# Two more blocks by seven products, and a block's second layer cut by unit halves, on one Trainium2 core

## The chip, the cores and the metric

The kernel runs on one core of a Trainium2 chip. Five engines matter: PE multiplies matrices and writes to PSUM, ACT and DVE do elementwise work and empty PSUM, POOL and SP here mostly issue DMAs. Each engine takes its own queue in order, and semaphores hold an instruction until what it needs is there. The metric is device time in microseconds (us) of one execution, as a median over runs.

## The reference

A gated recurrence over 6144 steps for each of 4 sequences and 256 channels, then a layer that takes the larger of two products and projects back:

```python
sig = 1.0 / (1.0 + np.exp(-f_logit))
f = lower_bound + (1.0 - lower_bound) * sig
h = f[:, t] * h + (1.0 - f[:, t]) * x[:, t]      # for each t; y[:, t] = h
g = np.maximum(y @ w1, y @ w2)                    # 256 -> 1024 units
out = g @ w_out                                   # 1024 -> 256
```

There are 24576 tokens in all, in fp32.

## The kernel before

**Algebra.** The larger of two products is written as max(a, b) = a + relu(b - a). So the first layer needs one product alone, with wd made from w2 - w1, and a ReLU; the part that stays linear goes through w13 = w1 w_out, a 256 x 256 matrix, added in the second layer. The factor of the recurrence's input (`om`, one minus the lower bound) is folded into the weights: `scale_w1` scales a half of w1, `half_w1` casts it to 16 bits, `make_wd` forms a quarter of wd, `turn_w1` and `keep_w1T` transpose the scaled w1 through PSUM, `make_w13` multiplies it by w_out (tile `wob`).

**Blocks.** Tokens are cut into 48 blocks of 512, the unit of all loops. A block has two SBUF tiles `r` (`rts[j, 0]` and `rts[j, 1]`), each with four 128-unit slices of the hidden layer and one slice with half of the recurrence's output y. The recurrence of a block: `gate` (sigmoid on ACT), `decay`, `drive` and two `scan`s on DVE, each scan starting from the end of the block before. `first_layer(j, fc)` makes unit slice fc with two matmuls of 512 columns; after each second slice ACT writes the ReLU of both to the `r` tile (L442). Its PSUM tile `dT` has two buffers of two banks each; all other PSUM tiles (`ps`) share four buffers of one bank.

**Second layer, direct.** `second_layer(j, slot)` issues an eighth of a block's 40 matmuls of 256 columns (L480): for each of four token groups two for y with w13 and eight for the units with w_out, y first. ACT or DVE copies the result out of PSUM (L489) and SP stores it.

**Second layer by sevens.** From block 4 on, two blocks are taken together as a 2 x 2 block product that needs seven products instead of eight: `sevenths(p)` lists 7 x 20 matmuls of 128 columns for pair p. For it DVE forms four sums of `r` tiles a pair (`sum1` to `sum4`, L499), and once four sums of weights (`make_sevens`). Products X, B and E are accumulated in PSUM banks; ACT copies one bank into another (`seed`), takes snapshots, and ACT or DVE writes the results (`leave`).

**Order.** The whole order is written by hand. Before the loop over pairs come the loads, the weights, and blocks 0 to 3 with their recurrences, each block's second layer set between the first-layer slices of the next. In the loop over p each of 16 slots issues a first-layer slice of pair p, then 8.75 of the list's matmuls of pair p - 1, and what `seq` and `gates` have due: scans and gates for pair p + 1, sums for p and p - 1. The list starts two slots late (`LAG`), in p = 3, so that 17.5 of a pair's matmuls are always left over to the next.

**Queues.** SP issues the first loads, the four weight loads, all stores, and `cross(c)`, the transposing loads of a chunk of 1024 tokens from a 16-bit scratch. POOL issues the casting loads: w_out, chunks 1 to 3 in natural layout (PE transposes them), and from chunk 4 on `fetch`, which writes the scratch; after `cross(c)` POOL waits for its first tile and then fetches chunk c + 1. POOL's first wait is `pool_waits(w1n[0])`: w_out and the fetches behind it are issued when the first half of w1 has landed.

## Time and profile before

| what | value |
|---|---|
| median of 5 runs | 378.79 us (378.07 to 380.32) |
| the profiled execution | 378.51 us |
| its span, first to last instruction | 376.7 us |
| PE busy | 369.4 us, 98% |
| DVE busy | 337.9 us, 90% |
| ACT busy | 303.2 us, 80% |
| granted clock of PE | 0.999 |
| w_out, issue to landing | 6.2 us |
| four loads of w1 and w2, issue to landing | 5.9 / 6.6 / 7.4 us (least, median, most) |

The span is the profiled execution from its first to its last instruction; the time also has 1.8 us around it. Busy shares are means over all stages. "Chain" means the work that ended last, followed back at each step to what released it. In a timeline row the first number is the start in us from the span's start, the second the time from the first start to the last end of a run of equal instructions; brackets hold the engine's idle time before it and what ended it. A matmul's duration includes the way through the array, so equal matmuls start closer together than they last.

### The profile page before, as it was taken

To read this page: it belongs to the slowest core of one execution; us is meant where nothing else is said; L and a number is where in the kernel's file an instruction comes from. 1 tells how busy PE (TensorE), PEld (TensorE's weight loads), DVE (VectorE), ACT (ScalarE), POOL (GpSimd) and SP (SyncE) were. 2 spreads that over 40 slices of the span, in tenths; PEclk is the share of its full clock that TensorE was granted. 3 is DMA by queue.
4 is the path that set the end of the run, shared out by engine and by line. 5 is a ranking of instruction groups with operands and counts; after the bars stand their busy time and mean duration, and the time that the engine had idled before them with its cause. 6 is when DMAs were issued, how large, how long until landed. Compare 5 with 4: busy or idle time off the path is not lost.

```text
span 376.7 us, 9634 instructions
## 1 busy us (share of the span) xinstructions
PE 369.4 (98%) x4156; PEld 281.9 (75%) x4156; DVE 337.9 (90%) x408; ACT 303.2 (80%) x412; POOL 36.8 (10%) x80
## 2 busy tenths in 40 slices
PE   7999999999999999999999999999999999999995
PEld 6777767777777777777777777777777777777784
DVE  5796889999999999999999999999999999999762
ACT  5866798888888798798888888887988888888752
POOL 1401100110110100110100201100101210000000
PEclk9999999999999999999999999999999999999999
DMA  7999989999999999998999979999989989920223
GB/s 264 241 198 247 220 155 201 212 214 214 264 203 205 250 177 227 260 180 224 276 150 244 278 141 235 298 160 234 278 143 252 278 159 229 229 114 2 114 113 112
DMA packets 104543, 77.17 MB, mean 205 GB/s; under 512 B 93298, under 2 KB 95348, under 8 KB 103796
## 3 DMA queue, kind: packets, MB, share of 16 engines
q1 hardware_dynamic: 101536, 51.19, 59.3%
q0 software_dynamic: 2544, 25.17, 34.8%
q8 instruction: 32, 0.52, 0.6%
q10 hardware_dynamic: 420, 0.20, 0.2%
q14 instruction: 11, 0.09, 0.1%
HBM read 53.48 MB, written 48.23 MB: 270 GB/s over the span
## 4 chain that ended last, share of the span: by engine, by line
PE 96%; DMA 2%; ACT 1%; SPq 0%; DVE 0%; issue 0%; DVEq 0%
PE ps L643 45%; PE dT L434 44%; PE ps L480 5%; DMA r<-in_moe_w_dram 2%; PE ps L174 1%; PE ps L390 0%; SPq L117 0%; ACT r L345 0%; ACT S L349 0%; PE ps L376 0%; DVE osb L561 0%; DVE osb L582 0%; ACT sn L574 0%; PE dT L643 0%; DVEq L561 0%
## 5 line engine op out<-in xcount | busy, mean ns | idle before, releaser
L442 ACT ACTIVATE r<-dT 128x1024 f16<-128x1024 f32 x192 | 195.9, 1023 | 53.5 <-PE dT L434 53.3
L434 PE MATMUL dT<-r,wd 128*128 128x512 f16 x768 | 225.0, 379 | 0.0
L643 PEld LDWEIGHTS <-S 128*128 128x128 f16 x1760 | 115.5, 101 | 37.2 <-DVE S L499 0.2
L643 PEld LDWEIGHTS <-r 128*128 128x128 f16 x1320 | 90.9, 101 | 36.8 <-issue 0.2
L224 DVE TENSOR_TENSOR_SCAN r<-ff,r,v 128x512 f16<-128x512 f16 x88 | 108.2, 1270 | 0.8
L643 PE MATMUL ps<-t,S 128*128 128x128 f16 x1320 | 101.6, 219 | 0.0
L499 DVE TENSOR_TENSOR S<-r 128x2560 f16<-128x2560 f16 x44 | 65.4, 1486 | 15.3 <-ACT r L442 15.3
L434 PEld LDWEIGHTS <-wd 128*128 128x128 f16 x768 | 67.6, 113 | 4.6 <-DVE wd L358 0.5
L643 PE MATMUL ps<-wob,r 128*128 128x128 f16 x704 | 69.9, 219 | 0.0
L499 DVE TENSOR_TENSOR S<-r,S 128x2560 f16<-128x2560 f16 x44 | 64.9, 1475 | 0.0
L279 ACT ACTIVATE u<-fT 128x512 f16<-128x512 f16 x88 | 56.1, 638 | 0.0
L207 DVE TENSOR_SCALAR ff<-u,nom 128x512 f16<-128x512 f16 (+1 forms) x98 | 31.6, 345 | 9.1 <-ACT u L201 3.1
L643 PE MATMUL ps<-w,r 128*128 128x128 f16 x176 | 38.5, 219 | 0.0
L341 POOL CAST waited<-fT 128x1 f32<-128x1 f16 x22 | 10.5, 477 | 275.5 <-DMA fT<-scr 275.5
L643 PE MATMUL ps<-t,r 128*128 128x128 f16 x430 | 34.1, 219 | 0.1
L561 DVE TENSOR_TENSOR osb<-ps,sn 128x512 f32<-128x512 f32 x44 | 30.1, 684 | 3.2 <-PE ps L643 3.2
L643 PE MATMUL ps<-wob,S 128*128 128x128 f16 x352 | 32.6, 219 | 0.0
L217 DVE TENSOR_TENSOR v<-u,xT 128x1024 f16<-128x1024 f16 x44 | 30.1, 684 | 0.0
L549 ACT COPY sn<-ps 128x512 f32<-128x512 f32 x44 | 25.8, 586 | 2.0 <-PE ps L643 2.0
L559 ACT COPY osb<-ps 128x512 f32<-128x512 f32 x43 | 25.1, 583 | 0.8 <-PE ps L643 0.8
L480 PEld LDWEIGHTS <-r 128*128 128x128 f16 x160 | 16.0, 101 | 6.6
L643 PE MATMUL ps<-w,S 128*128 128x128 f16 x88 | 19.3, 219 | 0.0
(58 smaller groups left out, 136.4 us busy)
## 6 DMA issues: line engine op xcount, KB each, us to landing
out_dram<-osb SPq DMA_DIRECT2D x46, 512.0 KB, 3.8
scr<-in_f_logit_dram POOLq DMA_DIRECT2D x22, 512.0 KB, 7.5
scr<-in_x_dram POOLq DMA_DIRECT2D x22, 512.0 KB, 10.0
r<-in_moe_w_dram SPq DMA_DIRECT2D x4, 512.0 KB, 6.6
fT<-in_f_logit_dram POOLq DMA_DIRECT2D x3, 256.0 KB, 8.2
xT<-in_x_dram POOLq DMA_DIRECT2D x3, 256.0 KB, 8.8
out_dram<-osb SPq DMA_DIRECT2D x3, 256.0 KB, 2.5
osb<-in_f_logit_dram SPq DMA_DIRECT2D x2, 256.0 KB, 3.7
```

What stands on the lines that cost most here:

```text
L207: nc.vector.tensor_scalar(out=ff[:, h, cols], in0=u[:, h, cols], scalar1=nom[:, h : h + 1], scalar2=1.0, op0=ALU.mult, op1=ALU.add,)
L217: nc.vector.tensor_tensor(out=like(v[:, :, cols], xT), in0=like(u[:, :, cols], xT), in1=xT, op=ALU.mult,)
L224: nc.vector.tensor_tensor_scan(out=y_of(j, h), data0=ff[:, h, o : o + TB], data1=v[:, h, o : o + TB], initial=0.0 if t0 == 0 else y_of(j - ...
L279: nc.scalar.activation(out=mids[p + NBLK, "u"][:, h, cols], in_=held[c, 0][:, h, cols], func=AF.Sigmoid, scale=-1.0,)
L434: nc.tensor.matmul(dT[:, fc % 2, :], lhsT=wd[:, kc, unit_cols(fc)], rhs=y_of(j, kc), start=(kc == 0), stop=(kc == KC - 1),)
L442: nc.scalar.activation(out=rts[j, k][:, g - 1 : g + 1, :].rearrange("p q (i m) -> p q i m", m=P), in_=dT[:].rearrange("p q (m i) -> p q i ...
L480: nc.tensor.matmul(ps[:, r, :], lhsT=left, rhs=right, start=(s == 0 and r == 0), stop=(s == n - 1 and r == 1), skip_group_check=True,)
L499: nc.vector.tensor_tensor(out=t[:], in0=a, in1=b, op=op)
L549: nc.scalar.copy(out=t[:], in_=bank[b][:])
L559: nc.scalar.copy(out=dst, in_=bank[b][:])
L561: nc.vector.tensor_tensor(out=dst, in0=bank[b][:], in1=snap[name][:], op=ALU.add)
L643: nc.tensor.matmul(bank[b][:, i, :], lhsT=a[:, k, cols], rhs=w, start=fresh, stop=after is not None, skip_group_check=True,)
```

## The change

- Blocks 2 and 3 become a pair of their own (p = 1) in the list of sevens, and are worked off beside the first layer of blocks 4 and 5 (p = 2). The list starts after one slot, so 8.75 matmuls are left over to each next pair instead of 17.5. Pair 1 has no seed: X is snapshotted, B gets a bank of its own, and DVE adds the snapshot at the end. The scans of blocks 4 to 7 move in the order.
- Block 1's second layer is set beside the first layer of blocks 2 and 3 (five and three pieces).
- w_out is loaded by two DMAs into two tiles, and POOL waits for the second cast of the first load (`raws[1, 1]`) instead of w1.
- Block 0's second layer is issued by unit halves into one PSUM tile `dT` that it keeps until the end (`second_first`): units 0 and 1 of all four token groups, then 2 and 3, later 4 to 7 and y. Its first layer for units 4 to 7 is made one by one in `ps` tiles (`first_single`), with ReLUs on ACT for 4 and 7 and on DVE for 5 and 6. ACT copies the four groups out at once.
- Scaling the second half of w1 moves from ACT to DVE; the two turns of w1 are further apart.

```diff
@@ -315,7 +314,7 @@
     lbr = const.tile([KC, P], FP32)
     waited = const.tile([P, 1], FP32)
     warm = const.tile([P, 1], FP32)
-    wob = wpool.tile([P, FC, D], HALF)
+    wob = [wpool.tile([P, KH, D], HALF, name=f"wob{g}") for g in range(2)]
     wd = wpool.tile([P, KC, DFF], HALF)
     w1T = wpool.tile([P, FC, D], HALF)
     w13 = wpool.tile([P, KC, D], HALF)
...
@@ -340,9 +339,9 @@
     def pool_waits(t):
         nc.gpsimd.tensor_copy(out=waited[:], in_=t)
-    def scale_w1(g):
+    def scale_w1(g, mul):
         for kc in range(KC):
-            nc.scalar.mul(w1s[g][:, kc, :], w1n[g][:, kc, :], om[:, kc : kc + 1])
+            mul(w1s[g][:, kc, :], w1n[g][:, kc, :], om[:, kc : kc + 1])
     def half_w1(g, copy):
         for kc in range(KC):
...
@@ -446,6 +445,29 @@
                 in_=dT[:].rearrange("p q (m i) -> p q i m", m=P),
                 func=AF.Relu,
             )
+
+    def first_single(fc, relu):
+
+        k, g = divmod(fc, KH)
+        dT = ps_o.tile([P, TB], FP32, name="ps")
+        for kc in range(KC):
+            nc.tensor.matmul(
+                dT[:],
+                lhsT=wd[:, kc, unit_cols(fc)],
+                rhs=y_of(0, kc),
+                start=(kc == 0),
+                stop=(kc == KC - 1),
+            )
+        relu(
+            out=rts[0, k][:, g, :].rearrange("p (i m) -> p i m", m=P),
+            in_=dT[:].rearrange("p (m i) -> p i m", m=P),
+        )
+
+    def relu_act(out, in_):
+        nc.scalar.activation(out=out, in_=in_, func=AF.Relu)
+
+    def relu_dve(out, in_):
+        nc.vector.tensor_scalar_max(out=out, in0=in_, scalar1=0.0)
     def store(j, osb, groups=slice(0, TB // P), cols=slice(0, D), queue=None):
         b, t0, nb, c, o = blocks[j]
...
@@ -486,11 +508,41 @@
                 skip_group_check=True,
             )
             if r == 1 and s == n - 1:
-                (nc.scalar.copy if j in (0, 3) else nc.vector.tensor_copy)(
+                (nc.vector.tensor_copy if j else nc.scalar.copy)(
                     out=osb[:, 2 * g : 2 * g + 2, :], in_=ps[:]
                 )
                 if i == ns - 1:
                     store(j, osb)
+
+    def second_first(i, fcs):
+
+        ns = TB // P
+        g, r = divmod(i, 2)
+        if "first" not in acc:
+            acc["first"] = ps_d.tile([P, 2, TB], FP32, name="dT")
+        ps = acc["first"][:, g, r * D : (r + 1) * D]
+        toks = slice(i * P, (i + 1) * P)
+        end = fcs[-1] == FC - 1
+        terms = [
+            (rts[0, fc // KH][:, fc % KH, toks], wob[fc // KH][:, fc % KH, :])
+            for fc in fcs
+        ]
+        terms += [(y_of(0, s)[:, i:TB:ns], w13[:, s, :]) for s in range(KC) if end]
+        for n, (left, right) in enumerate(terms):
+            nc.tensor.matmul(
+                ps,
+                lhsT=left,
+                rhs=right,
+                start=(fcs[0] == 0 and r == 0 and n == 0),
+                stop=(end and n == len(terms) - 1),
+                skip_group_check=True,
+            )
+        if end and i == ns - 1:
+            osb = opool.tile([P, ns, D], FP32, name="osb")
+            nc.scalar.copy(
+                out=osb[:].rearrange("p (g r) d -> p g (r d)", g=2), in_=acc["first"][:]
+            )
+            store(0, osb)
     sums = {}
...
@@ -601,8 +653,11 @@
         def given(t):
             return lambda k: t[:, k, :]
+
+
+        begin = p == PAIR0 - 1
         product("X", part(0, 0), plain(0, lo), True)
-        then(seed("B", "X"))
+        then(snapshot("X", 1) if begin else seed("B", "X"))
         product("E", sub(1), given(t1), True)
         then(snapshot("E", 5))
         if end:
...
@@ -623,8 +678,8 @@
         else:
             product("X", sub(2), given(t2))
             then(snapshot("X", 2))
-            product("B", part(0, 1), plain(1, lo))
-            then(leave("B", ja, lo, None, False))
+            product("B", part(0, 1), plain(1, lo), begin)
+            then(leave("B", ja, lo, 1 if begin else None, False))
             product("X", sub(3), given(t3))
             then(leave("X", jb, hi, 5, False))
             product("E", sub(4), plain(1, hi))
...
@@ -662,14 +717,6 @@
         fetch_first(1)
         for g in range(NG):
             fetch_w(g)
-        pool_waits(w1n[0][:, 0, 0:1])
-        nc.gpsimd.dma_start(
-            out=wob[:].rearrange("p (g q) c -> p g (q c)", g=NG),
-            in_=moe_w_out.rearrange("(g p q) c -> p g (q c)", g=NG, q=NQ),
-        )
-        for c in range(1, 5):
-            for s in range(2):
-                fetch(c, s)
         wt = ps_d.tile([P, 2, 2 * TB], HALF, name="dT")
         lbc = ps_d.tile([P, TB], FP32, name="dT")
...
@@ -694,81 +741,91 @@
         warm_up(8)
         first_bf16(1, 0, nc.scalar.copy)
         first_bf16(1, 1, nc.scalar.copy)
+        pool_waits(raws[1, 1][:, 0, 0:1])
+        for g in range(NG):
+            nc.gpsimd.dma_start(
+                out=wob[g][:].rearrange("p q c -> p (q c)"),
+                in_=moe_w_out[g * NQ * P : (g + 1) * NQ * P, :].rearrange(
+                    "(p q) c -> p (q c)", q=NQ
+                ),
+            )
+        for c in range(1, 5):
+            for s in range(2):
+                fetch(c, s)
         first_turn(1, 0)
         first_turn(1, 1)
         first_recurrence(1)
         warm_up(24)
-        scale_w1(0)
+        scale_w1(0, nc.scalar.mul)
         half_w1(0, nc.scalar.copy)
-        scale_w1(1)
         pt0 = turn_w1(0)
         for pair in range(2):
             make_wd(0, pair)
             for fc in range(2 * pair, 2 * pair + 2):
                 first_layer(0, fc)
+        scale_w1(1, nc.vector.tensor_scalar_mul)
         half_w1(1, nc.vector.tensor_copy)
-        pt1 = turn_w1(1)
         for pair in range(2):
             make_wd(1, pair)
-            for fc in range(4 + 2 * pair, 6 + 2 * pair):
-                first_layer(0, fc)
         keep_w1T(0, pt0)
-        keep_w1T(1, pt1)
+        for fcs in ((0, 1), (2, 3)):
+            for i in range(TB // P):
+                second_first(i, fcs)
+        keep_w1T(1, turn_w1(1))
+        first_single(4, relu_act)
+        first_single(5, relu_dve)
+        first_single(6, relu_dve)
         steps = turn_steps(1)
-        make_w13(0)
         turn(steps[:8])
         gate(1)
+        first_single(7, relu_act)
+        make_w13(0)
+        turn(steps[8:])
         make_w13(1)
-        turn(steps[8:])
         for step in scan_steps(1):
             step()
         cross(4)
-        for fc in range(FC):
-            if fc == 4:
-                turn(turn_steps(2))
-                gate(2)
-            if fc == 6:
-                first_layer(1, 0)
-                first_layer(1, 1)
-            if fc < 7:
-                second_layer(0, fc)
+        last = tuple(range(KH, FC))
+        steps = turn_steps(2)
+        second_first(0, last)
+        turn(steps[:8])
+        gate(2)
+        second_first(1, last)
+        second_first(2, last)
+        turn(steps[8:])
+        second_first(3, last)
         for step in scan_steps(2):
             step()
         for step in make_sevens():
             step()
-        for fc in range(2, FC):
+        for fc in range(FC):
             first_layer(1, fc)
             if fc == 3:
-                second_layer(0, 7)
-        turn(turn_steps(3))
+                turn(turn_steps(3))
         gate(3)
         cross(5)
-        early = scan_steps(3)
+        for step in scan_steps(3):
+            step()
+        scans = {PAIR0: pair_scans(PAIR0)}
+        part = 0
         for fc in range(FC):
             first_layer(2, fc)
-            second_layer(1, fc)
-            if fc < 4:
-                early[fc]()
+            if fc in (1, 2, 4, 5, 7):
+                second_layer(1, part)
+                part += 1
+            if fc > 3:
+                pair_gate(PAIR0, fc - 4)
+        for t in ("decay0", "drive0", "scan00", "scan01"):
+            scans[PAIR0][t]()
         cross(6)
-        scans = {PAIR0: pair_scans(PAIR0)}
-        gates = {0: 0, 1: 1, 4: 2, 5: 3}
-        order = {
-            2: ("decay0", "drive0"),
-            3: ("scan00",),
-            4: ("scan01",),
-            6: ("decay1",),
-            7: ("drive1",),
-        }
         for fc in range(FC):
             first_layer(3, fc)
-            second_layer(2, fc)
-            if fc in gates:
-                pair_gate(PAIR0, gates[fc])
-            for t in order.get(fc, ()):
-                scans[PAIR0][t]()
+            if fc in (1, 2, 4):
+                second_layer(1, part)
+                part += 1
+        sum3(1)
         queue, due = [], 0
-        pieces3, piece = (1, 3, 5, 9, 11, 13, 15), 0
         for p in range(PAIR0, NPAIR):
             first = p == PAIR0
             more = p + 1 < NPAIR
...
@@ -777,31 +834,30 @@
                 (36, scans[p]["scan11"]),
                 (112, lambda: sum3(p)),
             ]
+            if first:
+                seq += [(9, scans[p]["decay1"]), (10, scans[p]["drive1"])]
             if more:
                 scans[p + 1] = pair_scans(p + 1)
                 seq += [
-                    (64, scans[p + 1]["decay0"]),
-                    (66, scans[p + 1]["drive0"]),
-                    (70, scans[p + 1]["scan00"]),
-                    (84, scans[p + 1]["scan01"]),
+                    (73 if first else 64, scans[p + 1]["decay0"]),
+                    (75 if first else 66, scans[p + 1]["drive0"]),
+                    (79 if first else 70, scans[p + 1]["scan00"]),
+                    (93 if first else 84, scans[p + 1]["scan01"]),
                     (131, scans[p + 1]["decay1"]),
                     (133, scans[p + 1]["drive1"]),
                 ]
-            if not first:
-                seq += [
-                    (9, lambda: sum1(p - 1)),
-                    (18, lambda: sum2(p - 1)),
-                    (50, lambda: sum4(p - 1)),
-                ]
-                queue += sevenths(p - 1)
+            seq += [
+                (0 if first else 9, lambda: sum1(p - 1)),
+                (18, lambda: sum2(p - 1)),
+                (50, lambda: sum4(p - 1)),
+            ]
+            queue += sevenths(p - 1)
             seq.sort(key=lambda e: e[0])
-            gates = {4: 0, 6: 1, 12: 2, 14: 3} if more else {}
+            gates = {5 if first else 4: 0, 7 if first else 6: 1, 12: 2, 14: 3}
+            gates = gates if more else {}
             for slot in range(2 * FC):
                 first_layer(2 * p + slot // FC, slot % FC)
-                if first and slot in pieces3 or p == PAIR0 + 1 and slot == 1:
-                    second_layer(2 * PAIR0 - 1, piece)
-                    piece += 1
-                if p > PAIR0 + 1 or (p == PAIR0 + 1 and slot >= LAG):
+                if p > PAIR0 + 1 or slot:
                     due += NSEV / (2 * FC)
                     while due >= 1:
                         due -= 1
```

The remaining hunks put `wob[fc // KH][:, fc % KH, :]` where `wob[:, fc, :]` stood.

More of the change, by code (lines that the diff above doesn't have):

```diff
@@ L38 @@
     CH = 1024
-    LAG = 2
     NSEV = 7 * 4 * 5
@@ L392, in make_w13 @@
                 lhsT=w1T[:, fc, kc * P : (kc + 1) * P],
-                rhs=wob[:, fc, :],
+                rhs=wob[fc // KH][:, fc % KH, :],
                 start=(fc == 0),
@@ L403, in right @@
     def right(k, cols):
-        return wob[:, k * KH : (k + 1) * KH, cols], w13[:, k, cols]
+        return wob[k][:, :, cols], w13[:, k, cols]
     def make_sevens():
@@ L478, in second_layer @@
                 fc = s - KC
-                left, right = rts[j, fc // KH][:, fc % KH, toks], wob[:, fc, :]
+                left, right = rts[j, fc // KH][:, fc % KH, toks], wob[fc // KH][:, fc % KH, :]
             nc.tensor.matmul(
```

## The prediction

> **What bounds the kernel now.** I read the page's busy shares first, then the chain that ended last, then the timeline of the first 36 us and of the last 15, then busy time by stretches.
>
> ```profile
> span 376.7 us, 9634 instructions
> PE 369.4 (98%) x4156; PEld 281.9 (75%) x4156; DVE 337.9 (90%) x408; ACT 303.2 (80%) x412; POOL 36.8 (10%) x80
> PE 96%; DMA 2%; ACT 1%; SPq 0%; DVE 0%; issue 0%; DVEq 0%
> ```
>
> The matmul engine is the chain: from 11.5 us it has next to no gap until the last sums. So a change counts in two ways: by the matmuls that it removes, and by the waits that it puts in front of PE. The prices come from the chain's pieces in order of time (start, length, what):
>
> ```profile
> 11.50 1.73 PE dT L434 x8
> 21.28 1.09 PE ps L480 x10
> 58.77 0.50 PE ps L643 x9
> ```
>
> A 512-column matmul costs 0.216 us, a 256-column one 0.1095, a 128-column one 0.0557 (the last from a pair's 14.72 us less its 32 of 512: 7.80/140). The rows that feed PE, from the timeline, where the first number is the start and the second the duration:
>
> ```profile
> 8.64 0.87 POOL L666 DMA_DIRECT2D wob<-in_moe_w_out_dram  x1
> 12.13 0.75 DVE L349 CAST S<-r 128x512 f16<-128x512 f32 x2
> 12.40 1.94 ACT L442 ACTIVATE r<-dT 128x1024 f16<-128x1024 f32 x2
> 12.80 1.66 DVE L358 SCALAR_TENSOR_TENSOR wd<-r,om 128x256 f16<-128x256 f32 x4
> 14.39 1.28 DVE L382 COPY w1T<-ps 128x1024 f16<-128x1024 f16 x2
> ...
> 363.50 1.49 DVE L499 TENSOR_TENSOR S<-r 128x2560 f16<-128x2560 f16 x1
> ...
> 365.04 1.13 PEld L643 LDWEIGHTS <-S 128*128 128x128 f16 x20 [0.17 <-DVE S L499]
> ```
>
> The last row says that the final pair's product E already waits for its sum. And busy time by stretches of 5 us (after the length: PE, PEld, DVE, ACT, POOL with instruction counts, then granted clock, DMA share, GB/s):
>
> ```profile
> 10.00:15.00 5.00, 4.85 (x38) 3.08 (x36) 5.00 (x14) 4.53 (x7) 3.51 (x7) 1.00 1.10 246
> 15.00:20.00 5.00, 5.00 (x52) 4.27 (x51) 2.76 (x6) 3.10 (x5) 0.49 (x1) 1.00 1.12 209
> 35.00:40.00 5.00, 5.00 (x38) 3.74 (x37) 2.33 (x5) 4.05 (x6) 0.00 (x0) 1.00 0.71 127
> 50.00:55.00 5.00, 5.00 (x33) 3.29 (x32) 4.92 (x7) 4.82 (x7) 0.00 (x0) 1.00 0.68 117
> ```
>
> Over the nine stretches from 10 to 55 us DVE idles 8.7 us in all and ACT 10.2: that is the room for new side work.
>
> **The change, part by part.** I stepped the queues of PE, ACT and DVE through the order in which each program issues, with the rows' spacings: first-layer pair 0.87 on PE; ReLU of two units 0.92 apart on ACT; sums 1.40, scans 1.19 apart on DVE; 0.2 from a matmul's issue to its reader. The old order, stepped so, ends PE at 372.2; the trace has its last matmuls end there (371.49 + 0.72).
>
> 1. Matmuls. Blocks 2 and 3 cost 80 matmuls of 256 columns, 8.76 us; as sevens 140 of 128, 7.80. Gain 0.96. Block 0's second layer keeps its 40.
>
> 2. w_out. Its DMA leaves POOL after the cast that ends at 7.42 instead of after the first weight lands at 8.47. One issue of 128 rows takes 0.56 (the fetches behind it), so the halves are issued from about 7.65 and 8.2, and the eight fetches behind them 0.8 earlier. In the packet records w_out first moves at 10.87, 2.2 after its issue; so now at about 9.6. The four weight loads land at 8.47, 9.73, 11.00 and 12.34, so some 600 KB of them are still to come, chiefly w2's second half. Bounds for its landing: 12.34 if w_out yields, 16.3 if w_out goes wholly first (3.94 us from its first packet to its landing at 14.81). Where both overlap, about 11.2 to 11.5 us, a quarter microsecond holds 19 packets of w_out and 12 of the loads: neither goes first, so I take one for one: 300 packets of 2 KB at 0.08 + 0.17 us on 16 engines, 4.7 us, less the 0.2 or so that packets overlap: about 14.5. Half 0 of w_out then lands by some 12.5, ahead of its use at 13.4. Behind the new wait in POOL's queue stand both halves and the fetches; block 1's first transpose at 17.3 waits for them last, and since the same bytes go the same way, its tile still lands near 16.0. Were it late, PE would stand still by as much.
>
> The Trainium skill, "DMA: Bandwidth & Descriptors", section Queues, rings and completion order, says that each DMA engine takes turns between the queues it has work for, packet by packet. That agrees with these counts and speaks against an earlier w_out; by the rule the sum would be the one below, and without contention 0.7 less.
>
> 3. Weights of units 4 to 7. The two scalings move from ACT (0.72 each) to DVE. No row shows that operation on DVE; 0.35 (L207's 16-bit form) and 0.68 (L561) bound it, the cast L349 at 0.41 reads the same tile shape, so 0.41. DVE: wd of half 0 ends 12.15, scaling 12.97, cast 13.65; the second wd could start there and now waits for 14.5: 0.85 late, to 16.1; w1T copies 16.7 and 17.4 (L382, 0.64 each).
>
> 4. PE meanwhile: first layer of units 0 to 3 ends at 13.0. It used to go on with transposes; now block 0's second layer needs the ReLU of units 0 and 1, which ends at 13.42 (12.40 + 1.02): wait 0.41 with the second one's. Then 16 matmuls, transposes, units 4 and 5. Unit 6 needs a PSUM buffer that the first w1T copy frees, block 1's transposes the second's, unit 7 and w13 the buffers of units 5 and 6, whose ReLUs are on DVE (no row has it; L489 copies as much from PSUM in 0.68, 0.61 apart, L207 16-bit data in 0.35: I take 0.62, the PSUM row). Waits 0.34, 0.20, 0.17, 0.19 = 0.90 (0.22 with weights in time). The tail of block 0 waits 0.12 for w13's second copy (L397, 0.37).
>
> 5. Buffers. Block 0's accumulator holds one of the two first-layer PSUM buffers until ACT has copied it (nearest row L442, 1.02; 0.58 for half the size). Units 2 and 3 of block 1 wait 0.38 for it. Behind that copy ACT has four ReLUs and a gate in a row: first layer of block 2 waits 0.37, and of block 4 another 0.37, since block 3's stage has 3 pieces of second layer beside 8 units and so runs at ACT's pace.
>
> 6. Pair 1's sums. DVE gains four sums (5.6), three additions (1.8), scalings and ReLUs (2.1), and loses two output copies (1.2): some 8.3 us more by 58 us, against 8.7 idle. It is then full: sum 2 is 0.17 late for its product, y of block 5 0.13, and sum 1 of pair 2 0.44.
>
> 7. The loop. The list of sevens now runs 8.75 matmuls closer to its sums. In a steady pair sum 1 ends at 144.36 and E starts at 146.18; one slot earlier leaves 0.9 us, so nothing waits. ACT's seed becomes a snapshot of the same size once. At the end 9 matmuls instead of 18 cover the last sum, so the 0.11 there becomes 0.61: 0.50 lost. Transposing loads, their SP queue (block 1's store goes behind chunk 6's load; its buffer is next needed 8 us later) and the fetches are hidden: chunk 5 lands at 43.1, its gate is due near 46; beyond 3 us of delay the next pair's scans, then its first layer, would slip.
>
> Sum: waits 0.41 + 0.90 + 0.12 + 0.38 + 0.37 + 0.37 + 0.74 + 0.50 = 3.79; less 0.96; less 0.6 of small waits that the same stepping puts into the old order between 12 and 19 us and that go: **+2.2 us**. The profiled execution took 378.51 (span 376.7 and 1.8 around it); with the sum 380.7. It lies 0.3 below the median 378.79, so I forecast 381.0.
>
> **Rivals.**
> - Weights in time (half 1 of w2 by 13.65): point 4 loses 0.7, sum +1.5, 380.3. For it: w_out's packets may start later than 9.6. Against: they need a delay of over a microsecond.
> - w_out first: landing 16.3, unit 4 itself waits; +4.0, 382.8. The counts in the overlap speak against it.
> - Not slower: ACT hides the hand-overs. If ReLU and copy leave their buffers early enough, the waits of points 4 and 5 (2.18) and of 6 (0.74) do not form, and -0.96 + 0.50 gives 378.3. It decides at 1.6 us of new waits ahead of the tail (I have 2.7 there after the 0.6 taken off): below that the time is not slower by 0.3%, about what a measurement here can tell. For it: ACT idles 1.9 us from 15 to 20 and 2.7 from 30 to 35 now. Against: the order puts each ReLU directly before its reader at 13.4, and DVE's 2.7 idle us from 35 to 40 are spent by point 6.
> - DVE never catches up: later than 0.9 us in every pair, E waits each time. At 0.1 a pair 2 us more, 383. DVE is 95% busy in the loop, with 0.56 idle before sum 3 in each pair; that works the lag off in about three pairs, so I hold it unlikely.
>
> **How the numbers follow.** Late weights with all waits 0.40; weights in time 0.27, of which 0.07 ends inside 0.3%; w_out first or a lasting lag 0.10; waits mostly hidden 0.23, of which 0.16 inside 0.3% and 0.07 faster by more. So slower 0.70, the same 0.23, faster 0.07: the saving itself is 0.96, under the 1.14 that counts. The range 378.9 to 383.0 reaches from half-hidden waits to w_out first.
>
> **What would show it.** After: PE with gaps at 13.0 (released by ACT's ReLU), 16 to 18.7 (DVE's copies and ReLUs), near 25 and 29 (ACT); wd of half 1 starting near 14.5 after an idle of DVE released by a weight DMA; DVE over 4.8 of 5 us in each stretch from 20 to 55; PE waiting 0.6 for the last sum 1. If PE has under 1.6 us of new gaps before 60 us, I am wrong.

## The result and the profile after

The changed kernel takes 380.17 us (median of 22 runs, 379.43 to 381.62) against 378.57 for the kernel before on the same chip (41 runs, 377.85 to 380.52): a ratio of 1.004, 95% interval 1.003 to 1.0051. Its profiled execution took 380.4 us, span 378.5; 1.9 more than the one of before. The predicted 381.0 was 0.8 high, the range 378.9 to 383.0 holds the result, and the sign is the predicted one.

From the page of the changed kernel: the span, the busy shares and the chain that ended last.

```profile
span 378.5 us, 9765 instructions
PE 369.5 (98%) x4216; PEld 281.5 (74%) x4216; DVE 345.6 (91%) x417; ACT 302.2 (80%) x411; POOL 41.2 (11%) x81
PE 94%; DMA 3%; ACT 1%; SPq 0%; DVE 0%; issue 0%; POOL 0%; DVEq 0%
```

PE issues 60 matmuls more (140 small ones for 80 larger) and is as busy as before, yet its last matmul ends at 374.04 instead of 372.21 us, 1.83 later. The chain gives up two points of PE, one of them to DMA: on the page it now leads through the landing of w_out (2%). The busy time of PE includes some of a wait, since a matmul counts until it leaves the array, so below a **gap** is the time between the starts of two matmuls less the spacing of that shape (0.0557, 0.1095 or 0.2165 us). Bracketed idle time in a row is about 0.16 shorter than the gap.

The timeline of the changed kernel (start, duration, engine and line, what, and in brackets the idle time before it with what ended it):

```profile
7.67 1.22 POOL L746 DMA_DIRECT2D wob<-in_moe_w_out_dram  x2
...
8.92 1.34 ACT L344 ACTIVATE r<-r,om 128x512 f32<-128x512 f32 x2 [0.96 <-DMA r<-in_moe_w_dram]
...
11.98 0.88 DVE L344 TENSOR_SCALAR r<-r,om 128x512 f32<-128x512 f32 x2
...
12.83 1.94 ACT L441 ACTIVATE r<-dT 128x1024 f16<-128x1024 f32 x2 [1.54 <-PE dT L433]
13.44 1.67 DVE L357 SCALAR_TENSOR_TENSOR wd<-r,om 128x256 f16<-128x256 f32 x4
...
14.15 1.91 PE L532 MATMUL dT<-wob,r 128*128 128x256 f16 x16 [0.50 <-DMA wob<-in_moe_w_out_dram]
...
17.41 1.29 DVE L470 TENSOR_SCALAR r<-ps 128x512 f16<-128x512 f32 x2 [0.17 <-PE ps L454]
...
24.50 1.01 ACT L542 COPY osb<-dT 128x1024 f32<-128x1024 f32 x1 [1.39 <-PE dT L532]
...
25.56 1.02 PE L433 MATMUL dT<-r,wd 128*128 128x512 f16 x4 [0.24 <-ACT osb L542]
...
29.45 1.02 PE L433 MATMUL dT<-r,wd 128*128 128x512 f16 x4 [0.25 <-ACT r L441]
...
41.14 1.02 PE L433 MATMUL dT<-r,wd 128*128 128x512 f16 x4 [0.25 <-ACT r L441]
...
42.03 1.49 DVE L551 TENSOR_TENSOR S<-r 128x2560 f16<-128x2560 f16 x1 [0.31 <-ACT r L441]
...
366.87 1.13 PEld L698 LDWEIGHTS <-S 128*128 128x128 f16 x20 [0.17 <-DVE S L551]
```

Four things are to be seen. The predicted hand-overs stand at 14.15, 25.56, 29.45 and 41.14, the first released by w_out and not by the ReLU (which ended at 13.85). The second `wd` starts at 13.44 with no wait for a weight. DVE idles for 0.31 us ahead of pair 1's sum 1, until ACT's ReLU is done. And the last pair's product E waits 0.17 for its sum, exactly as before: nothing was lost at the end.

Busy time by stretches of the changed kernel (PE, PEld, DVE, ACT, POOL, then clock, DMA share, GB/s):

```profile
10.00:15.00 5.00, 3.76 (x30) 2.30 (x28) 5.00 (x13) 3.23 (x5) 2.58 (x5) 1.00 1.11 243
...
25.00:30.00 5.00, 4.51 (x33) 2.64 (x32) 4.72 (x11) 4.08 (x5) 0.00 (x0) 1.00 0.57 65
30.00:35.00 5.00, 5.00 (x35) 3.46 (x33) 3.70 (x5) 4.68 (x7) 1.15 (x3) 1.00 1.41 311
...
40.00:45.00 5.00, 4.75 (x46) 3.11 (x44) 4.69 (x7) 3.95 (x5) 1.04 (x2) 1.00 1.04 194
```

PE loses time in the stretches of those hand-overs, at an undisturbed clock. DVE is busy 4.9 us more over 10 to 55 us, and still idles 1.3 us in one stretch (30 to 35): it is fuller, not full.

All gaps of PE, term by term as the prediction set them up:

| term | predicted | measured |
|---|---|---|
| matmuls | -0.96 | -0.96 |
| before block 0's second layer | 0.41 | 0.66 at 13.3 us |
| DVE's copies and ReLUs, 16 to 18.7 us | 0.90 | 0 |
| w13's second copy | 0.12 | 0.08 at 21.2 |
| block 0's accumulator | 0.38 | 0.40 at 25.0 |
| ReLU before block 2 | 0.37 | 0.41 at 28.8 |
| ReLU before block 4 | 0.37 | 0.41 at 40.5 |
| sum 2; y of block 5 | 0.17; 0.13 | 0.15; 0.11 at 45.9, 48.2 |
| sum 1 of the next pair | 0.44 | 0 |
| a bank, and y of block 7 | - | 0.09 and 0.18 at 54.5, 62.6 |
| last sum 1 | 0.50 | 0 |
| small waits of before that go | -0.6 | -0.16 |
| first half of w1 landing later | - | 0.43 |
| sum | +2.2 | +1.80 |

The sum of the gaps, 1.80, accounts for nearly all of the 1.83 by which the last matmul is later.

### The profile page after: what moved, and what is told of

Same layout as the page of the kernel before. It is cut to its first block, busy times and chain, and to the rows that moved or that the text cites. A ratio compares the mean times of both kernels' runs of the same rounds, so it can differ in the third digit from the quotient of the medians.

```text
span 378.5 us, 9765 instructions
## 1 busy us (share of the span) xinstructions
PE 369.5 (98%) x4216; PEld 281.5 (74%) x4216; DVE 345.6 (91%) x417; ACT 302.2 (80%) x411; POOL 41.2 (11%) x81
## 3 DMA queue, kind: packets, MB, share of 16 engines
q0 software_dynamic: 2560, 25.17, 34.7%
## 4 chain that ended last, share of the span: by engine, by line
PE 94%; DMA 3%; ACT 1%; SPq 0%; DVE 0%; issue 0%; POOL 0%; DVEq 0%
PE ps L698 47%; PE dT L433 42%; DMA wob<-in_moe_w_out_dram 2%; PE dT L532 1%; DMA osb<-in_x_dram 1%; PE ps L502 1%; PE ps L173 1%; ACT r L441 1%; PE ps L389 0%; PE ps L454 0%; SPq L116 0%; ACT osb L542 0%; DVE osb L613 0%; ACT nat L127 0%; DVE osb L634 0%
## 5 line engine op out<-in xcount | busy, mean ns | idle before, releaser
L441 ACT ACTIVATE r<-dT 128x1024 f16<-128x1024 f32 x190 | 193.9, 1022 | 52.3 <-PE dT L433 52.2
L698 PEld LDWEIGHTS <-S 128*128 128x128 f16 x1840 | 120.8, 101 | 39.3 <-issue 0.3
L698 PEld LDWEIGHTS <-r 128*128 128x128 f16 x1380 | 95.1, 101 | 38.7 <-issue 0.5
L698 PE MATMUL ps<-t,S 128*128 128x128 f16 x1380 | 106.4, 219 | 0.0
L551 DVE TENSOR_TENSOR S<-r 128x2560 f16<-128x2560 f16 x46 | 68.4, 1486 | 14.9 <-ACT r L441 14.8
L698 PE MATMUL ps<-wob,r 128*128 128x128 f16 x736 | 73.1, 219 | 0.0
L551 DVE TENSOR_TENSOR S<-r,S 128x2560 f16<-128x2560 f16 x46 | 67.9, 1476 | 0.0
L340 POOL CAST waited<-fT 128x1 f32<-128x1 f16 x22 | 14.7, 670 | 274.1 <-DMA fT<-scr 274.1
L613 DVE TENSOR_TENSOR osb<-ps,sn 128x512 f32<-128x512 f32 x47 | 32.1, 683 | 3.2 <-PE ps L698 3.2
L595 ACT COPY ps<-ps 128x512 f32<-128x512 f32 x22 | 12.5, 570 | 3.3 <-PE ps L698 0.6
```

Source lines behind the costliest of these rows:

```text
L340: nc.gpsimd.tensor_copy(out=waited[:], in_=t)
L441: nc.scalar.activation(out=rts[j, k][:, g - 1 : g + 1, :].rearrange("p q (i m) -> p q i m", m=P), in_=dT[:].rearrange("p q (m i) -> p q i ...
L551: nc.vector.tensor_tensor(out=t[:], in0=a, in1=b, op=op)
L613: nc.vector.tensor_tensor(out=dst, in0=bank[b][:], in1=snap[name][:], op=ALU.add)
L698: nc.tensor.matmul(bank[b][:, i, :], lhsT=a[:, k, cols], rhs=w, start=fresh, stop=after is not None, skip_group_check=True,)
```

## The experiments

The theory was that the change is two changes with a price each: hand-overs between PE and ACT (or DVE) that the new order leaves without other work for PE. The rivals were an earlier w_out that takes bandwidth from the weights, and a DVE that falls behind.

### Which half costs

**The sevens alone.** The parts for blocks 2 and 3 in the kernel before, whose start and single w_out DMA stay:

```diff
         for fc in range(FC):
             first_layer(2, fc)
-            second_layer(1, fc)
+            if fc in (1, 2, 4, 5, 7):
+                second_layer(1, part)
...
         for fc in range(FC):
             first_layer(3, fc)
-            second_layer(2, fc)
+            if fc in (1, 2, 4):
+                second_layer(1, part)
+        sum3(1)
...
-            if not first:
-                queue += sevenths(p - 1)
+            queue += sevenths(p - 1)
```

> Blocks 2 and 3 as sevens, with the old start (one w_out DMA, block 0 as before). If the time is PE's matmuls and gaps: 0.96 us fewer matmuls, against the gaps of the changed kernel that lie behind 40 us (0.41 + 0.15 + 0.11 + 0.09 = 0.76), so -0.2 us against the kernel before, 378.4, not to be told from it. If pair 1's extra sums overload DVE, or if the new start is what makes room for them, PE has over 2 us of gaps behind 40 us and the time is 379.8 or more.

379.28 us against 378.64, ratio 1.0009 (0.9986 to 1.0032). The gaps in its profile: 0.41 before block 4, 0.15, 0.10, 0.44 (a bank that DVE reads late), 0.18, and at the start 0.22 and 0.36 behind a w_out that landed at 15.5 us. The first of them, and the sum that follows:

```profile
39.95 1.02 PE L434 MATMUL dT<-r,wd 128*128 128x512 f16 x4 [0.25 <-ACT r L442]
...
40.85 1.49 DVE L499 TENSOR_TENSOR S<-r 128x2560 f16<-128x2560 f16 x1 [0.31 <-ACT r L442]
```

So the 0.96 of fewer matmuls is paid back here too, and the expected 378.4 did not come. The same program once more, to see how much of that is scatter:

> The sevens alone once more, to stand beside the spread version on the same chip. Its first profile had chunk 5 land at 46.6 us, 3 us later than in the kernel before, with ACT waiting 0.37 us for it and 0.44 us of gap at the bank that DVE then reads late. If that is scatter of the DMA chain, this profile has the chunk before 45 and that gap under 0.15; if the earlier sevens bring it about, it stays. Time 378.4 to 379.3.

379.26 against 378.95, ratio 1.0012 (0.9998 to 1.0026). The bank now cost 0.09 instead of 0.44, and the start nothing; the 0.41, 0.15, 0.10 and 0.18 stayed. This execution lost 1.30 and 0.41 in the middle of the loop instead, at 171 and 231 us, each time because DVE waited for an earlier store to land before it could write the next output. The first:

```profile
171.69 0.69 DVE L561 TENSOR_TENSOR osb<-ps,sn 128x512 f32<-128x512 f32 x1 [1.88 <-DMA out_dram<-osb]
...
172.44 0.27 PE L644 MATMUL ps<-t,r 128*128 128x128 f16 x2 [1.14 <-DVE osb L561]
```

That store took 12.3 us from issue to landing; the median of these stores in the kernel before is 3.8. The four gaps that stay and the bank's 0.09 sum to 0.93, against the 0.96: that half gains nothing.

**The start alone.** The new start with blocks 2 and 3 worked off directly:

```diff
+    LAG = 2
...
-        for step in scan_steps(3):
-            step()
+        early = scan_steps(3)
...
-            if fc in (1, 2, 4, 5, 7):
-                second_layer(1, part)
+            second_layer(1, fc)
+            if fc < 4:
+                early[fc]()
```

> The new start alone (two w_out DMAs, block 0's second layer by unit halves), blocks 2 and 3 direct. If the gaps of the start are its cost: 0.43 (first w1 half lands later) + 0.66 (w_out's first half) + 0.08 + 0.40 (accumulator) + 0.41 (ReLUs of block 1) less 0.11 that goes = +1.9 us, 380.4. If the start only looks bad beside the sevens, which fill DVE and ACT, it stays within 0.5 us of the kernel before, 379.1 at most.

379.87 against 378.64, ratio 1.0025 (1.0008 to 1.0043). The expected 380.4 had counted 0.43 for a late w1, which did not recur (8.36 us). Its timeline shows the same three waits as the full change up to 30 us, and PE has no gap between 30 us and the last sums:

```profile
13.61 1.91 PE L533 MATMUL dT<-wob,r 128*128 128x256 f16 x16 [0.50 <-DMA wob<-in_moe_w_out_dram]
...
25.01 1.02 PE L434 MATMUL dT<-r,wd 128*128 128x512 f16 x4 [0.24 <-ACT osb L543]
...
28.91 0.59 PE L434 MATMUL dT<-r,wd 128*128 128x512 f16 x2 [0.25 <-ACT r L442]
```

The two halves add up: 1.2 us for the start and 0.3 to 0.6 for the sevens, against 1.6 together. Most of the loss is the start's, by the gaps too: 1.55 us there against 0.93 less the 0.96 saved.

### Hand-overs with nothing between

**Work moved to the bare places.** The transposes of block 3 in two halves behind block 1's units 1 and 7, and block 1's last pieces spread over block 3's stage:

```diff
-            if fc == 3:
-                turn(turn_steps(3))
+            if fc == 1:
+                steps = turn_steps(3)
+                turn(steps[:8])
+            if fc == 7:
+                turn(steps[8:])
...
-            if fc in (1, 2, 4):
+            if fc in (1, 4, 7):
```

> The changed kernel with other work set into three hand-overs: block 3's transposes in halves after block 1's units 1 and 7 instead of together after unit 3, and block 1's last pieces after block 3's units 1, 4 and 7 instead of 1, 2 and 4. If the three gaps of 0.40 to 0.41 are PE waiting for one ReLU or copy to leave a PSUM buffer, each is covered by 0.45 or 0.55 us of work: -1.2 us, 379.0. If ACT is what is short there, the gap moves to the next first-layer slice and the time stays at 380.0 or above.

381.29 against 378.64, ratio 1.0067 (1.0044 to 1.009): slower than the change. The waits moved instead of going:

```profile
27.60 1.02 PE L433 MATMUL dT<-r,wd 128*128 128x512 f16 x4 [0.23 <-ACT r L441]
...
37.81 0.59 PE L433 MATMUL dT<-r,wd 128*128 128x512 f16 x2 [0.29 <-ACT r L441]
...
40.83 0.69 DVE L511 COPY osb<-ps 128x512 f32<-128x512 f32 x1 [1.76 <-PE ps L502]
...
44.37 0.51 PE L698 MATMUL ps<-t,S 128*128 128x128 f16 x6 [0.74 <-DVE S L551]
...
46.91 0.34 PE L698 MATMUL ps<-t,S 128*128 128x128 f16 x3 [0.38 <-DVE S L551]
```

The gaps at 25.0, 28.8 and 40.5 are gone, but one of 0.40 stands where the transposes had been taken from, and one of 0.45 between two pairs of units that lost their piece. DVE idled for 1.76 us in front of the copy of the late piece, which stood in its queue ahead of `sum3` and `sum1`, and E waited 0.91 and the next product 0.54 for the sums behind it. A piece used as cover has a reader, and that reader has a queue.

**Something behind every pair of units.** Both halves of the transposes, one piece ahead of block 2, and the rest evenly; `sum3` ahead of the last pieces:

```diff
+            if fc == 1:
+                steps = turn_steps(3)
+                turn(steps[:8])
             if fc == 3:
-                turn(turn_steps(3))
+                turn(steps[8:])
+        second_layer(1, 0)
...
-            if fc in (1, 2, 4, 5, 7):
+            if fc in (1, 3, 5, 7):
...
-            if fc in (1, 2, 4):
+            if fc == 3:
+                sum3(1)
+            if fc in (1, 3, 5):
...
-        sum3(1)
```

> The changed kernel with something behind every pair of units: block 3's transposes in halves after block 1's units 1 and 3, block 1's pieces before block 2, after units 1, 3, 5, 7 of block 2 and 1, 3, 5 of block 3, and pair 1's first sum after unit 3 of block 3. If each 0.4 us gap is a hand-over with no work between, all three go and w_out's gap in the start and 0.4 us of late sums stay: 379.0. If they come back elsewhere: 380.0 or more.

379.36 against 378.95, ratio 1.001 (0.9998 to 1.0023). All three gaps of 0.4 are gone (0.12 and 0.08 remain near 35 us); what remains large is w_out and sum 2, whose gap grew from 0.15 to 0.51:

```profile
13.41 1.91 PE L532 MATMUL dT<-wob,r 128*128 128x256 f16 x16 [0.38 <-DMA wob<-in_moe_w_out_dram]
...
40.65 1.49 DVE L551 TENSOR_TENSOR S<-r 128x2560 f16<-128x2560 f16 x1
...
44.72 0.34 PE L698 MATMUL ps<-t,S 128*128 128x128 f16 x3 [0.35 <-DVE S L551]
```

This is the fastest form of the whole change that was run. By the medians it recovers about 1.2 of the 1.6 us (0.4 above the kernel before is left), by the gaps 0.8 (1.71 of new ones instead of 2.49); the rest is within the scatter. It shows that the gaps of 0.4 came from pairs of units with nothing between them.

**The same on the old start**, against the sevens alone:

```diff
-            if fc in (1, 2, 4):
+            if fc == 3:
+                sum3(1)
+            if fc in (1, 3, 5):
...
-        sum3(1)
```

> The sevens of blocks 2 and 3 with the old start; in block 3's stage block 1's last pieces stand after units 1, 3 and 5 (one behind each pair of units, instead of after 1, 2 and 4), and pair 1's first sum is issued after unit 3, ahead of the copy behind the last piece. If the 0.41 us in front of block 4 is one ReLU that PE must wait out when nothing stands between two pairs of units, it goes, and the gaps left behind 38 us are 0.15 + 0.10 + 0.18 and at most 0.1 more: 0.96 - 0.5 gives 378.2, a little under the kernel before. If the wait moves to sum 1 or to another ReLU, as when the last piece stood after unit 7, PE keeps 0.9 us or more of gaps there and the time is 378.6 to 379.3.

379.06 against 378.95, ratio 1.0003 (0.9987 to 1.0019): no difference, where 378.2 had been expected if the gap simply went. The 0.41 before block 4 is gone, and sum 2 waits 0.51 here as well:

```profile
40.50 1.49 DVE L499 TENSOR_TENSOR S<-r 128x2560 f16<-128x2560 f16 x1 [0.63 <-ACT r L442]
...
44.58 0.34 PE L644 MATMUL ps<-t,S 128*128 128x128 f16 x3 [0.35 <-DVE S L499]
```

Sum 1 starts when block 3's last ReLU is done; decay, drive and sum 2 follow it on DVE. Is it DVE's load or that ReLU which makes sum 2 late? Take one copy off DVE:

```diff
-                (nc.scalar.copy if j in (0, 3) else nc.vector.tensor_copy)(
+                (nc.scalar.copy if j == 0 or g else nc.vector.tensor_copy)(
```

> The spread version with the old start, and block 1's second output copy (0.68 us on DVE) on ACT. In the spread version 0.51 us of PE's gap stands in front of the product that needs sum 2. If DVE's queue ahead of sum 2 makes it (first sum, copy, sum 1, decay, drive), the gap falls to 0.1 or less and the time is 378.5, 0.4 under the kernel before. If sum 2 waits for ReLUs of block 3, it stays near 0.5 and the time at 378.9 to 379.1.

379.39 against 378.93, ratio 1.0011 (0.998 to 1.0042). Sum 2's gap stays 0.51, and DVE now idles longer in front of sum 1:

```profile
40.40 1.49 DVE L499 TENSOR_TENSOR S<-r 128x2560 f16<-128x2560 f16 x1 [1.22 <-ACT r L442]
```

So sum 1 is held by block 3's last ReLU and not by DVE's earlier work, and decay, drive and sum 2 stand behind it in DVE's order: 0.36 of the 0.41 saved before block 4 comes back there.

**Two earlier tries** at the same place, both on the sevens alone. Block 1's copies all on ACT:

```diff
-                (nc.scalar.copy if j in (0, 3) else nc.vector.tensor_copy)(
+                nc.scalar.copy(
```

> As the sevens alone, but block 1's two output copies (0.68 us each) go from DVE to ACT. If DVE's load makes the late gaps (0.15 for sum 2, 0.10 for block 5's y, 0.44 at a bank that DVE has to read, 0.18 for block 7), they fall to 0.3 in all or less, and the 0.41 in front of block 4 stays: 378.7. If ReLU and sum latency make them, they stay as they are: 379.2.

380.05 against 378.84, ratio 1.0023 (1.0002 to 1.0045). The late gaps are as in the second run of the sevens (0.16, 0.10, 0.09, 0.18), so DVE's copies do not make them. A gap of 0.37 behind ACT is new at 36 us, the one before block 4 stays at 0.47, and this execution also lost 0.45 and 0.37 at the start, behind a w_out that landed at 15.81. And with those copies on ACT, nine matmuls of the list set before block 4:

```diff
         queue, due = [], 0
+        queue += sevenths(1)
+        for _ in range(9):
+            queue.pop(0)()
+        due = -0.25
```

> The sevens of blocks 2 and 3 with the old start, block 1's output copies on ACT, and the first nine matmuls of the list in front of block 4's first layer instead of in slot 1. If the gaps are what eats the 0.96 us: the 0.41 in front of block 4 is covered by 0.50 us of matmuls and the DVE gaps shrink with its load, so PE has under 0.5 us of gaps from 38 to 64 us and the time is 378.1, half a microsecond under the kernel before. If a gap only moves to the next ReLU or sum, it is 378.8 or more.

379.54 against 378.84, ratio 1.0022 (1.0 to 1.0044). The 0.41 before block 4 is gone, but 0.37 stands at 34.7 us, sum 2 waits 0.54, and a bank that DVE reads late costs 1.12 at 52.9 us, after ACT had waited for chunk 5:

```profile
46.80 0.63 ACT L279 ACTIVATE u<-fT 128x512 f16<-128x512 f16 x1 [1.59 <-DMA fT<-scr]
...
54.06 0.27 PE L644 MATMUL ps<-t,r 128*128 128x128 f16 x2 [0.96 <-DVE osb L561]
```

Moving the copies brings a wait at the other engine and shortens none. Chunk 5 landed about 2 us or more later in this profile and in the first of the sevens (46.7 and 46.5 us) than in any other: its transposing load took 7.6 and 6.4 us to land, against 4.8 to 5.4. Why was not settled.

### w_out

**POOL waits for w1 as before**, with everything else as in the change:

```diff
-        pool_waits(raws[1, 1][:, 0, 0:1])
+        pool_waits(w1n[0][:, 0, 0:1])
```

> The changed kernel, but POOL waits for the first half of w1 again before it issues w_out. If w_out yields to the weight loads whenever it is issued, its first half lands within 0.3 us of 14.0 as now, and if the early issue is what delays w1 by 0.43 that goes: 379.7 to 380.0. If the earlier issue brings the landing forward one for one, it now lands near 15.0, PE waits about 1.6 us instead of 0.66 in front of block 0's second layer, and the time is 381.0.

379.81 against 378.64, ratio 1.0037 (1.002 to 1.0055), as the change itself. In its profiled execution w1 landed at 7.64, so w_out left at 7.86, hardly later than in the change, and this run separates little: first packet 10.29, landing 12.75, and a gap of 0.42 before the second layer, which is the ReLU's. Its median is 1.2 above the kernel before, the change's 1.6: a gain from the earlier release cannot be read from it.

**Let go still earlier**, behind the second cast of the recurrence's first inputs:

```diff
-        pool_waits(raws[1, 1][:, 0, 0:1])
+        pool_waits(raws[0, 1][:, 0, 0:1])
```

with that wait, the two DMAs and the fetches set ahead of `first_turn(0, 0)`.

> The changed kernel, with w_out and the fetches behind it let go about 3 us earlier, after the second cast on DVE (4.6 us). If the DMA engines share one for one between the loads and w_out, as the prediction has it, w_out's first packet moves near 7.5 us, w2's second half lands 4 us or more later than 12.3, and PE waits for it: 383 or more. If w_out's packets come only where the loads have drained, its first packet stays at 10 us or later and w2's landing within 1 us: 380.2.

382.86 against 378.84, ratio 1.0103 (1.007 to 1.0136). DVE's rows of the start:

```profile
14.13 0.90 DVE L344 TENSOR_SCALAR r<-r,om 128x512 f32<-128x512 f32 x2 [1.81 <-DMA r<-in_moe_w_dram]
...
18.06 1.67 DVE L357 SCALAR_TENSOR_TENSOR wd<-r,om 128x256 f16<-128x256 f32 x4 [2.37 <-DMA r<-in_moe_w_dram]
```

In the profiled execution (384.6; the four runs range from 382.2 to 384.6) w_out first moved at 8.99, its half 0 landed at 11.97, the weights' second half at 14.11 (w1) and 17.59 (w2), and PE stood still for 2.43 us before unit 4. Block 0's second layer waited 0.42, for the ReLU alone, so 0.25 of the change's 0.66 there is w_out's. From 9.5 to 14.5 us each half microsecond holds 29 to 35 packets of 2 KB of w_out and the fetches beside 30 to 38 of the weight loads: one for one. This is the lateness that the prediction's point 2 described; the change itself did not reach it.

### Block 0's accumulator

Its copy shared by ACT and DVE, a half each:

```diff
-            nc.scalar.copy(
-                out=osb[:].rearrange("p (g r) d -> p g (r d)", g=2), in_=acc["first"][:]
-            )
+            whole = osb[:].rearrange("p (g r) d -> p g (r d)", g=2)
+            nc.scalar.copy(out=whole[:, 0, :], in_=acc["first"][:, 0, :])
+            nc.vector.tensor_copy(out=whole[:, 1, :], in_=acc["first"][:, 1, :])
```

> The changed kernel, with block 0's accumulator copied out by ACT and DVE at once, half each, instead of by ACT alone in 1.0 us. If the 0.40 us in front of block 1's third unit is the length of that copy, it falls under 0.05 and the time to 379.8. If DVE takes the copy only when its scans let it, the gap stays or grows: 380.2 or more.

380.22 against 378.84, ratio 1.0033 (1.0015 to 1.0051). The gap grew from 0.40 to 0.70:

```profile
24.39 0.69 DVE L544 COPY osb<-dT 128x512 f32<-128x512 f32 x1 [1.36 <-ACT osb L543]
...
25.14 1.02 PE L433 MATMUL dT<-r,wd 128*128 128x512 f16 x4 [0.54 <-DVE osb L544]
```

DVE was idle for 1.36 us and started its half at 24.39, when ACT's was done at 24.35: the halves ran one after the other, 0.58 and 0.69 instead of 1.01 in one piece. So the buffer came free later, and not because DVE was busy. Why DVE's copy waits for ACT's, which shares its input and output tile, was not looked into, and two halves at the same time remain untried.

## Why the prediction was right, and where it was not

The main case, late weights with all waits, did not happen; 380.17 is nearest to the 380.3 of the rival "weights in time", though not by that rival's terms.

**Right, with its mechanism:** point 1 (0.96), the accumulator and the two ReLUs of point 5 (1.12 predicted, 1.22 measured; removed by the spread order, moved by the first try at cover). One reason in it does not hold: block 3's stage does not run at ACT's pace, since ACT is busy for 4.33 and 3.95 of 5 us there, and the same three pieces in other places remove the gap before block 4. The rival "ACT hides the hand-overs" fell: it was decided at 1.6 us of new waits, and there are 2.5, with 0.16 of old ones gone. (The 2.18 that it names for points 4 and 5 leaves out one of the two 0.37; they add to 2.55.)

**Points 2 and 3, the weights: wrong.** The step that failed is "in the packet records w_out first moves at 10.87, 2.2 after its issue; so now at about 9.6". It takes the 2.2 for a constant. In the changed kernel w_out moves at 10.48, 2.8 after its issue at 7.67; by then 0.26 MB of the weights were left, w2's second half was there by 13.3, ahead of the 13.44 at which DVE had its turn, and nothing shared with it for long. (Two sums of that point are off besides: 7.65 and 2.2 make 9.85, and 9.6 and 4.7 less 0.2 make 14.1.) So the 0.90 of point 4 did not form: the rival "weights in time" held for the weights, and even its remaining 0.22 did not show. Over the fourteen profiles it took 1.6 to 4.0 us from issue to first packet. In six of them w_out left at 7.62 to 7.72 and first moved at 10.04 to 10.56; in five it left at 8.43 to 8.82 and first moved at 10.20 to 10.87: about 1 us earlier out, 0.2 us earlier under way. The delay grew with the weights still to come (1.6 to 2.4 us with 0.9 to 1.1 MB, 2.3 to 2.9 with 1.2 to 1.4 MB, 4.0 with 2.2 MB when it left at 4.97), but what sets it was not tried by itself. The rule cited from the Trainium skill, "DMA: Bandwidth & Descriptors", section Queues, rings and completion order, that an engine alternates between its queues packet by packet, agrees with the counts of the run that let w_out go still earlier; it spoke of an overlap that the change had for the last 0.26 MB of the weights alone.

**Point 4, first wait: right place, another releaser.** 0.41 was the ReLU's; measured 0.66, since w_out's half 0 landed at 14.02, 0.17 behind the ReLU. Of the 1.5 by which the term "by some 12.5" failed, 0.9 is that first packet; the other 0.6 came between first packet and landing, 3.5 us instead of the 2.9 taken.

**Point 7, the end: wrong.** "The list of sevens now runs 8.75 matmuls closer to its sums" misreads the loop. In `if p > PAIR0 + 1 or slot` the first slot is left out in p = 2 and again in p = 3, so from there on 17.5 matmuls stay over, as in the kernel before; the description of the change ahead of the prediction has the same error. Hence the 0.17 before the last E in both kernels, and the 0.50 that was not lost. (Its "0.11 there" is also misread: the row that the prediction shows has 0.17.)

**Point 6, sum 2 and block 5's y: right size, wrong reason.** 0.30 predicted, 0.26 measured, but not because DVE was full: it idled for 0.31 us ahead of sum 1, which waited for block 3's last ReLU, and decay, drive and sum 2 follow in its queue. That the size fits is luck. "DVE over 4.8 in each stretch from 20 to 55" fails in three of the seven.

**Point 6, sum 1 of the next pair:** 0.44 predicted, none found. The count of DVE's work was nearly right: up to the start of that sum DVE is busy 7.7 us more (43.92 from 10 to 57.65 us, against 36.18 from 10 to 54.85). So the sum starts 2.8 us later, but E, which needs it, starts 1.64 later too (59.48 instead of 57.84). The margin between the sum's end and E shrank from 1.50 to 0.35 and was not used up.

**The 0.6 of old waits:** the kernel before had only 0.16 of gaps there that the change removes. The stepping model put waits into the old order that its trace doesn't have.

**Not foreseen:** 0.27 of small waits at 54 and 62 us, and 0.43 because w1's first half landed at 8.90 instead of 8.47. The latter is scatter between executions: over the fourteen profiles it landed between 7.54 and 8.90, and in each of them before w_out's first packet moved.

So the total is nearer than its parts, and that is luck: 1.84 us of waits did not come (0.90, 0.50, 0.44), and 1.4 of other time did or failed to go (0.25 for w_out, 0.43, 0.27, and 0.44 of the 0.6).

## What to carry to other kernels

Where PE is the chain, a reordering is worth its matmuls less every hand-over that it lays bare: two pairs of first-layer units with nothing between cost 0.4 us here, so three of them ate more than 140 smaller products saved. Something between them removes the gap only if its own reader, and the queue that this reader stands in, is not late for something else; look for the next chain of latencies (here last ReLU, sum, decay, drive, sum) before counting the gain. And read loop conditions for every value of the loop variable when a list's lead is at stake.

## What was not expected of the hardware

From the issue of w_out on POOL to its first packet it took 1.6 to 4.0 us, longest where the most of the weight loads was still to come, so the instant of issue is a poor guide to when it begins to compete. Scaling an fp32 tile of 128x512 took DVE 0.44, and the ReLU of a 128x512 tile out of PSUM 0.65, both within 0.03 of what was predicted from the nearest rows. Single stores took 10 to 13 us to land instead of 3.8, in every profile; in one execution DVE had to wait for two of them, which cost PE 1.30 and 0.41 us. The transposing loads scatter as well, with a median of 2.6 us and single ones of 4 to 7 us in every profile, mostly without a gap of PE behind them.

No version tried is faster than the kernel before. Open are what sets the delay of w_out's first packet, and what makes a store or a transposing load late.
